# Attention by head pairs: block-diagonal keys and values, the bias factor in its band, and casts on GpSimd

## The chip, the cores and the metric

The kernel runs on one core of a Trainium2 chip. The metric is the device time of one execution in microseconds (us). The core has five engines that run side by side, each with an instruction queue of its own that is worked off in order: TensorE (PE in the profile, with its weight loads as PEld), VectorE (DVE), ScalarE (ACT), GpSimd (POOL) and SyncE (SP). SP, ACT and POOL can also start DMA transfers, which 16 DMA engines carry out.

## What is computed

Attention with a relative bias over 8 batches of 8 heads, 576 positions, head size 64, and behind it a mixture of experts in which a hash of the token's id picks one of 8 experts. Cut to what matters:

```python
scores = (1 / sqrt(D)) * q @ k.T + bias_table[bucket(|i - j|)]   # 8 x 8 heads, 576 x 576
attn = softmax(scores)                                           # over the keys j
x = (attn @ v), heads side by side                               # 4608 tokens x 512
e = token_ids * 2654435761 % 8                                   # one expert for each token
out[token] = relu(x[token] @ w1[e]) @ w2[e]                      # 512 -> 1024 -> 512
```

The bucket of a distance |i - j| grows up to 128, from there on it is the last one. Both kernels compute exp(score) times exp(bias), take the sum of a row from a column of ones beside the values, and divide at the end.

## The kernel before

**Setup** (lines 121 to 228). `tok`, `ident`, the one-hot table `ohsb` and the ids are loaded; a matmul makes the bias of every distance, ACT takes its exponential (`ebsb`), and it goes to DRAM (`t_ebp`). The token's rank within its expert is found by matmuls with a triangle and with ones; the result `ds2` is the row of `t_xperm` to which the token's `x` is to go. ACT's queue writes 5,140 KB of a fixed row over all expert slots of `t_xperm` (`zx`, line 301).

**Attention** (lines 232 to 430) runs over 8 batches `b` and in them over 4 head pairs `m`. SP loads `v` in float32 (`vb`), POOL loads `q` and `k` with a cast to float16 (`qb16`, `kb16`), 128 positions by 8 heads at a time. For each head a bias factor `ebias[h]` of 128 x 5 x 576 is read from DRAM, by way of a second DRAM array (`t_ebr`), in the first batch (`load_ebias`). For a pair PE transposes q and k (`psq`, `psk`), DVE copies them to `qT` and `kT` and casts v into `vaug` with its column of ones. The keys are cut into 5 tiles `t` of 128, 128, 128, 128 and 64. For each tile PE makes the scores of both heads (line 352: 64 rows of the array for a head, columns 512 and 64), ACT the exponential (line 360, 576 columns), DVE the product with `ebias` (line 368, 576 columns). Then for each head (line 393) 25 matmuls of 65 columns sum attn times v over the 5 key tiles for 5 chunks of queries; DVE takes reciprocals (line 406) and scales into `x_sb` (line 411). After a batch POOL sends 4 or 5 tiles of `x_sb` to their rows of `t_xperm` (line 420, "the dispatch").

**Experts** (lines 436 to 516): for each expert 640 rows are loaded from `t_xperm` (`xpn`, SP), transposed (`xps`), multiplied by `w1t` (`hps`, 512 matmuls of 320 columns in all) and `w2t` (`ops`, 320 of 512 columns), and POOL scatters the rows to the output. The change leaves these lines as they are. A branch behind them, for experts with over 640 tokens, is not entered.

What sets the order: the tile framework places the instructions of each engine in an order of its own and puts in the waits. Each DMA counts one of eight counters of its kind when it lands: `DMAHW0` to `DMAHW7` in turn for those from SP and ACT, `DMASW0` to `DMASW7` for those from POOL. The issue that comes to a counter again waits until the DMA before it on that counter has landed, and everything behind that issue in the same queue waits with it.

## Time and profile before

| | us |
|---|---|
| median of 3 runs | 644.87 (643.94 to 645.23) |
| the profiled execution | 647.33 |
| its span | 645.5 |
| PE busy | 526.1 |
| DVE busy | 315.6 |
| ACT busy | 245.3 |
| POOL busy | 159.3 |

The span is the stretch that the profile covers, and the sums below are made against it; the profiled execution took 1.8 us more than its span, the median 0.6 us less. A busy share is a mean over three stages with different limits: the setup up to about 96 us, the attention up to about 471 us, the experts behind it. So the profile is read stage by stage: what the chain of waits goes through there, and how long one instruction takes there.

### The profile page before, as it was taken

Reading aid. Unit: us, or ns where it says so; the run is one execution under the profiler, and the core shown is the slowest. Engines: PE = TensorE matmul, PEld = TensorE weight load, DVE = VectorE, ACT = ScalarE, POOL = GpSimd, SP = SyncE. Lnnn points to the kernel's source line nnn. Section 1 sums busy time; section 2 is a strip of 40 time slices with the busy share of each in tenths; the row PEclk is TensorE's granted clock in tenths of the full one; section 3 lists DMA queues with packets and bytes.
Section 4 is the critical chain, followed back from the end, with each engine's and each line's share of the span. In section 5 each row is a group of like instructions: output and inputs, shape, how many; then the busy total and the mean of one; then the engine's idle time right before and its main releaser. Section 6 shows DMA issues by size and latency. Waiting matters only on the chain.

```text
span 645.5 us, 9277 instructions
## 1 busy us (share of the span) xinstructions
PE 526.1 (82%) x3561; PEld 278.4 (43%) x3561; DVE 315.6 (49%) x1126; ACT 245.3 (38%) x386; POOL 159.3 (25%) x176
## 2 busy tenths in 40 slices
PE   2005149999999999999999999999919999999993
PEld 0002024454454454454454454454416655556661
DVE  0112036677676677676667666667612223322211
ACT  1004024445445445445545545545503322223330
POOL 5015310022232222232222330020020334423222
PEclk9999999999999999999999999999999999999997
DMA  9999999702912902911901910000032999999812
GB/s 149 184 152 164 235 269 246 167 35 18 130 43 13 134 34 14 135 42 11 136 34 11 137 43 1 1 34 1 1 95 79 196 218 212 218 187 205 183 73 82
DMA packets 147414, 69.74 MB, mean 108 GB/s; under 512 B 115155, under 2 KB 138743, under 8 KB 147360
## 3 DMA queue, kind: packets, MB, share of 16 engines
q0 software_dynamic: 92480, 40.40, 45.6%
q1 hardware_dynamic: 49744, 23.39, 16.2%
q10 hardware_dynamic: 5136, 5.26, 4.3%
q8 instruction: 30, 0.49, 0.3%
q14 instruction: 24, 0.20, 0.1%
HBM read 75.79 MB, written 22.99 MB: 153 GB/s over the span
## 4 chain that ended last, share of the span: by engine, by line
PE 63%; DMA 14%; issue 9%; ACT 8%; DVE 3%; POOL 1%; POOLq 0%; SPq 0%
PE px L393 21%; PE sc L352 14%; PE hps L478 11%; PE ops L496 11%; ACT attn L360 8%; DMA t_xperm<-zx 7%; PE psq L314 3%; DVE attn L368 2%; DMA ebias<-t_ebr 2%; PE psk L314 2%; DMA t_ebp<-ebsb 2%; PE xps L459 2%; DMA t_ebr<-t_ebp 1%; DMA vb<-in_v_dram 1%; POOL t_xperm L420 1%
## 5 line engine op out<-in xcount | busy, mean ns | idle before, releaser
L360 ACT ACTIVATE attn<-sc 128x576 f16<-128x576 f32 (+1 forms) x320 | 197.7, 648 | 257.0 <-PE sc L352 246.1
L393 PE MATMUL px<-vaug,attn 128*128 128x65 f16 (+3 forms) x1600 | 182.1, 243 | 24.7 <-DVE attn L368 22.0
L352 PE MATMUL sc<-qT,kT 64*128 64x512 f16 (+3 forms) x640 | 177.8, 428 | 22.9 <-ACT attn L360 22.6
L368 DVE TENSOR_TENSOR attn<-attn,ebias 128x576 f16<-128x576 f16 (+1 forms) x320 | 139.5, 452 | 93.4 <-ACT attn L360 56.0
L393 PEld LDWEIGHTS <-attn 128*128 128x128 f16 (+3 forms) x1600 | 117.4, 122 | 130.3 <-DVE attn L368 81.8
L484 ACT ACTIVATE h<-hps 128x640 f16<-128x640 f32 x64 | 45.1, 704 | 115.4 <-PE hps L478 115.0
L420 POOL DMA_INDIRECT t_xperm<-x_sb,ds x36 | 38.4, 1066 | 198.7 <-DVE x_sb L411 190.2
L352 PEld LDWEIGHTS <-kT 64*128 64x128 f16 (+1 forms) x640 | 46.6, 116 | 78.2 <-issue 68.0
L496 PE MATMUL ops<-w2t,h 128*128 128x512 f16 x320 | 72.7, 379 | 0.0
L478 PE MATMUL hps<-xpt,w1t 128*128 128x320 f16 x512 | 71.9, 301 | 0.0
L411 DVE TENSOR_SCALAR x_sb<-px,rcp 128x64 f16<-128x64 f32 (+1 forms) x320 | 70.0, 274 | 1.6
L274 POOL DMA_DIRECT2D qb<-in_q_dram x40 | 35.1, 878 | 131.1 <-PE psk L314 102.6
L478 PEld LDWEIGHTS <-w1t 128*128 128x128 f16 x512 | 50.4, 98 | 21.0 <-issue 0.2
L314 PE MATMUL psq<-ident,qb 128*128 128x128 f16 (+1 forms) x160 | 36.1, 292 | 21.9 <-DMA qb<-in_q_dram 15.2
L504 POOL DMA_INDIRECT out_dram<-ok,xpn x40 | 39.3, 981 | 56.5 <-DVE ok L503 54.4
L463 DVE COPY xpt<-xps 128x640 f16<-128x640 f16 x32 | 15.1, 489 | 73.6 <-PE xps L459 72.6
L503 DVE COPY ok<-ops 128x512 f32<-128x512 f32 x40 | 27.7, 692 | 47.0 <-PE ops L496 47.0
L314 PE MATMUL psk<-ident,kb 128*128 128x128 f16 (+1 forms) x160 | 36.5, 297 | 12.4 <-DMA kb<-in_k_dram 12.4
L496 PEld LDWEIGHTS <-h 128*128 128x128 f16 x320 | 30.7, 98 | 33.5
L406 DVE RECIPROCAL rcp<-px 64x1 f32<-64x1 f32 (+1 forms) x128 | 18.7, 166 | 50.6 <-PE px L393 47.8
L278 POOL DMA_DIRECT2D kb<-in_k_dram x40 | 35.2, 879 | 33.0 <-DMA kb<-in_k_dram 18.3
L314 PEld LDWEIGHTS <-qb 128*128 128x128 f16 (+1 forms) x160 | 19.8, 131 | 43.0 <-issue 26.1
(47 smaller groups left out, 138.6 us busy)
## 6 DMA issues: line engine op xcount, KB each, us to landing
vb<-in_v_dram SPq DMA_DIRECT2D x32, 256.0 KB, 5.1
w1t<-in_moe_w_dram POOLq DMA_DIRECT2D x8, 1024.0 KB
w2t<-in_moe_w_dram POOLq DMA_DIRECT2D x8, 1024.0 KB
ebias<-t_ebr SPq DMA_DIRECT2D x8, 720.0 KB, 7.5
t_xperm<-zx ACTq DMA_DIRECT2D x1, 5140.0 KB, 44.3
xpn<-t_xperm SPq DMA_DIRECT2D x8, 642.5 KB, 9.3
qb<-in_q_dram POOLq DMA_DIRECT2D x32, 128.0 KB
kb<-in_k_dram POOLq DMA_DIRECT2D x32, 128.0 KB
```

The costliest lines, as they stand in the source:

```text
L278: nc.gpsimd.dma_start(out=kb16[:nt, t, :, :], in_=k[b, :, P * t : P * t + nt, :].transpose([1, 0, 2]),)
L314: nc.tensor.transpose(out=pst[:, P * t : P * t + nt], in_=srct[:nt, t, 2 * m : 2 * m + 2, :], identity=ident[:nt, :nt],)
L352: nc.tensor.matmul(out=scps[hh][:nt, ns:ne], lhsT=kT[64 * hh : 64 * hh + 64, P * t : P * t + nt], rhs=qT[64 * hh : 64 * hh + 64, ns:ne], s ...
L360: nc.scalar.activation(out=attn[hh][:nt, t, :], in_=scps[hh][:nt, :], func=AF.Exp, bias=0.0, scale=scale,)
L368: nc.vector.tensor_tensor(out=attn[hh][:nt, t, :], in0=attn[hh][:nt, t, :], in1=ebias[2 * m + hh][:nt, NJT - 1 - t, :], op=ALU.mult,)
L393: nc.tensor.matmul(out=px[nbase : nbase + isz, c, :], lhsT=attn[hh][:nt, t, i0c : i0c + isz], rhs=vaug[hh][:nt, t, :], start=(imm == 0), s ...
L411: nc.vector.tensor_scalar(out=x_sb[nbase : nbase + isz, gt, h * D : (h + 1) * D], in0=px[nbase : nbase + isz, c, :D], scalar1=rcp[nbase : ...
L420: sc_in = nc.gpsimd.indirect_dma_start(out=xperm_d.ap()[:, :], out_offset=bass.IndirectOffsetOnAxis(ap=ds2[:, g : g + 1], axis=0), in_=x_s ...
L478: nc.tensor.matmul(out=hps[:, nr, :NR], lhsT=w1h[:, kt, ts(ft, P)], rhs=xt[e][:, kt, ts(nr, NR)], start=(kt == 0), stop=(kt == NPT - 1),)
L484: nc.scalar.activation(out=h1[:, ft, :].rearrange("p (r n) -> p r n", r=NRC), in_=hps[:, :, :NR], func=AF.Relu, bias=0.0, scale=1.0,)
L496: nc.tensor.matmul(out=ops[:, :], lhsT=h1[:, ft, ts(kc, P)], rhs=w2h[:, ft, :], start=(ft == 0), stop=(ft == NFT - 1),)
L504: so = nc.gpsimd.indirect_dma_start(out=out[:, :], out_offset=bass.IndirectOffsetOnAxis(ap=xn[e][:, kc, DM:XW].bitcast(I32), axis=0), in_= ...
```

## The change

Attention is written anew; the experts are not touched.

- **Pairs and block-diagonal keys.** `load(n)` loads q, k and v of one pair in float32 by eight DMAs of SP's queue; `cast_qk` and `cast_v` cast them to float16 on GpSimd. q and k are split into even and odd positions. `transposes(n)` makes 12 transposes of 96 x 128; DVE copies q to `qt`, and the keys of the two heads into the two diagonal blocks of `kz` (its other blocks are set to zero once). So one matmul with 128 rows gives the scores of 64 keys of either head: nine key tiles in all, eight of them taken in four groups `g` of 2 x 576 columns, and one of 576 (`scores`).
- **Values.** `va` holds the values of both heads in the same way, each head with its column of ones and zeros in the other's rows. Attn times v (`av_steps`) is 45 matmuls of 128 x 128 by 130 columns for a pair, in two PSUM tiles `px` of 27 and 18.
- **Bias in its band.** Distances of 128 and more have the last bucket; its factor cancels in the division. The table holds exp(bias - last bias), and DVE multiplies only the band around the diagonal: 7 operations with 512, 768, 512, 256, 256, 384 and 192 elements of a partition. Its table `ebd` is loaded by 16 DMAs, eight from SP and eight from ACT.
- **Order.** PE's order is written out: the scores of pair n between blocks of 12 matmuls of attn times v of pair n-1, and at the end the transposes of pair n+2. PSUM has two buffers `ps` of three banks, and two of one bank (`aux`) that `pq`, `pk` and `px` take in turn.
- **Dispatch.** 40 tiles go to `t_xperm`, five for each batch; routing (`route`) moves behind the second pair.

```diff
-                nc.gpsimd.dma_start(
-                    out=qb16[:nt, t, :, :],
-                    in_=q[b, :, P * t : P * t + nt, :].transpose([1, 0, 2]),
-                )
...
+        def aux(shape, dtype, name):
+            return atp.tile(shape, dtype, name=name, tag="aux", bufs=2,
+                            space=bass.MemoryType.PSUM)
...
+        kz = [at.tile([P, NCH, 2, D], F16, name=f"kz{i}") for i in range(3)]
+        va = [at.tile([P, NCH, VW], F16, name=f"va{i}") for i in range(4)]
+        ebd = at.tile([P, NPAIR, 2, 2, WB], F16, name="ebd")
...
+        def load(n):
+            b, m = pairs[n]
+            for dst, src, name in ((qf, q, "qf"), (kf, k, "kf")):
+                dst[n] = at.tile([PB, 2, NBLK, 2 * D], F32, name=name, bufs=4)
+                for hh in range(2):
+                    nc.sync.dma_start(
+                        out=dst[n][:, hh, :, :],
+                        in_=src[b, 2 * m + hh].rearrange(
+                            "(k p c) d -> p k (c d)", k=NBLK, c=2
+                        ),
+                    )
+            vf[n] = at.tile([P, NCH, D], F32, name="vf", bufs=4)
+            for hh in range(2):
+                for c in range(2):
+                    r0 = D * hh + HD * c
+                    nc.sync.dma_start(
+                        out=vf[n][r0 : r0 + HD, :, :],
+                        in_=v[b, 2 * m + hh].rearrange(
+                            "(x p c) d -> c p x d", c=2, p=HD
+                        )[c],
+                    )
+
+        def cast_qk(n):
+            for dst, src, name in ((qh, qf, "qh"), (kh, kf, "kh")):
+                dst[n] = at.tile([PB, 2 * NBLK, 2, D], F16, name=name, bufs=3)
+                nc.gpsimd.tensor_copy(
+                    out=dst[n][:, :, :, :].transpose([0, 2, 1, 3]),
+                    in_=src[n][:, :, :, :].rearrange(
+                        "p h k (c d) -> p h (k c) d", c=2
+                    ),
+                )
+
+        def cast_v(n):
+            for hh in range(2):
+                r0, r1 = D * hh, D * hh + D
+                nc.gpsimd.tensor_copy(
+                    out=va[n % 4][r0:r1, :, hh * (D + 1) : hh * (D + 1) + D],
+                    in_=vf[n][r0:r1, :, :],
+                )
+
+        for n in range(2):
+            load(n)
+
+        tbl = at.tile([NB, H], F32, name="tbl")
+        nc.sync.dma_start(out=tbl[:, :], in_=bias_table)
+        ohsb = at.tile([NB, FW], F32, name="ohsb")
+        nc.scalar.dma_start(out=ohsb[:, :], in_=OH_d.ap())
+        nc.sync.dma_start(out=ident[:, :], in_=I128_d.ap())
...
+        for i, x in enumerate(va):
+            for hh in range(2):
+                r0, r1 = D * hh, D * hh + D
+                o0, o1 = D - D * hh, P - D * hh
+                c0 = hh * (D + 1)
+                nc.gpsimd.memset(x[o0:o1, :, c0 : c0 + D + 1], 0.0)
+                nc.gpsimd.memset(x[r0:r1, :, c0 + D : c0 + D + 1], 1.0)
+            if i < 2:
+                cast_v(i)
...
+        nc.gpsimd.memset(zx[:, :DM], 0.0)
+        nc.gpsimd.memset(zx[:, DM:XW].bitcast(I32), BIG)
+
+        def fill_table():
+            nc.scalar.dma_start(
+                out=xperm_d.ap()[:NSLOT, :].rearrange("(p r) d -> p r d", p=P),
+                in_=zx[:, :].unsqueeze(1).to_broadcast([P, NSLOT // P, XW]),
+            )
+
...
+        def transposes(n):
+            b, m = pairs[n]
+            pq = aux([P, S], F16, "pq")
+            pk = aux([P, S], F16, "pk")
...
+            qt = at.tile([P, S], F16, name="qt", bufs=3)
+            nc.vector.tensor_copy(out=qt[:, :], in_=pq[:, :])
+            z = kz[n % 3]
+            for hh in range(2):
...
+        def scores(n, g):
+            b, m = pairs[n]
+            qt, z = qts[n], ktz[n]
+            ps = atp.tile([P, 3, 512], F32, name="ps", bufs=2,
+                          space=bass.MemoryType.PSUM)
+            if g == 0:
+                atts[n] = (
+                    at.tile([P, NDUO, 3, QW], F16, name="att", bufs=3),
+                    at.tile([P, S], F16, name="atts", bufs=3),
+                )
+            att, ats = atts[n]
+            if g < NDUO:
+                for c in range(2):
+                    kt = z[:, 2 * g + c, :, :].rearrange("p h u -> p (h u)")
+                    nc.tensor.matmul(
+                        out=ps[:, c, :QW], lhsT=kt, rhs=qt[:, :QW],
+                        start=True, stop=True,
+                    )
+                    nc.tensor.matmul(
+                        out=ps[:, 2, RW * c : RW * c + RW], lhsT=kt,
+                        rhs=qt[:, QW:], start=True, stop=True,
+                    )
+                nc.scalar.activation(
+                    out=att[:, g, :, :], in_=ps[:, :, :QW],
+                    func=AF.Exp, bias=0.0, scale=scale,
+                )
...
+                    nc.vector.tensor_tensor(
+                        out=a, in0=a,
+                        in1=ebd[:, m, :, :, a0 + w0 : a1 + w0], op=ALU.mult,
+                    )
...
+        def av_steps(n):
+            b, m = pairs[n]
+            att, ats = atts[n]
+            vb = va[n % 4]
+            for its in ((0, 1, 2), (3, 4)):
+                px = aux([P, len(its), 2, D + 1], F32, "px")
+                todo = [(ii, it, t) for ii, it in enumerate(its)
+                        for t in range(2 * NDUO + 1)]
+                for x, (ii, it, t) in enumerate(todo):
...
+                    nc.tensor.matmul(
+                        out=px[:, ii, :, :].rearrange("p h d -> p (h d)"),
+                        lhsT=lhsT, rhs=vb[:, t, :],
+                        start=(x == 0), stop=(x == len(todo) - 1),
+                        skip_group_check=True,
+                    )
+                    if x < len(todo) - 1:
+                        yield
+                ni = len(its)
+                rcp = at.tile([P, 3, 2], F32, name="rcp", bufs=4)
+                nc.vector.reciprocal(out=rcp[:, :ni, :], in_=px[:, :, :, D])
+                nc.vector.tensor_tensor(
+                    out=x_all[:, b, its[0] : its[0] + ni,
+                              P * m : P * m + P].rearrange(
+                        "p t (h d) -> p t h d", h=2
+                    ),
+                    in0=px[:, :, :, :D],
+                    in1=rcp[:, :ni, :].unsqueeze(3).to_broadcast(
+                        [P, ni, 2, D]
+                    ),
+                    op=ALU.mult,
+                )
+                yield
...
+        def dispatch(b):
+            for t in range(NIT):
                 sc_in = nc.gpsimd.indirect_dma_start(
                     out=xperm_d.ap()[:, :],
                     out_offset=bass.IndirectOffsetOnAxis(
+                        ap=ds2[:, B * t + b : B * t + b + 1], axis=0
                     ),
+                    in_=x_all[:, b, t, :],
                     in_offset=None,
+                    bounds_check=NROW - 1,
+                    oob_is_err=False,
                 )
                 disjoint(sc_in, "xrows")
+
+        def advance(it, count):
+            for _ in range(count):
+                if next(it, "end") == "end":
+                    return
+
+        NP = len(pairs)
+        with tc.manual_schedule(engines={mybir.EngineType.PE}):
+            transposes(0)
+            transposes(1)
+            for n in range(NP + 1):
+                av = av_steps(n - 1) if n > 0 else iter(())
+                if n < NP:
+                    if n + 2 < NP:
+                        load(n + 2)
+                        cast_qk(n + 2)
+                        cast_v(n + 2)
+                    for g in range(NIT):
+                        scores(n, g)
+                        if g < NDUO:
+                            advance(av, 12)
+                    advance(av, 99)
+                    if n + 2 < NP:
+                        transposes(n + 2)
+                    if n == 1:
+                        fill_table()
+                        route()
+                    if n == 4 * 5:
+                        load_w1(0)
+                        load_w2(0)
+                else:
+                    advance(av, 99)
+                if n > 0 and pairs[n - 1][1] == NPAIR - 1:
+                    dispatch(pairs[n - 1][0])
+            load_w1(1)
+            load_w2(1)
```

How the framework places this shows at three places. The first is SP's queue at the start; names in square brackets are the counters waited for. Before:

```order
L142 DMA sltsb<-t_slt 128x128
L148 DMA er<-in_moe_token_ids_dram 36x256
L268 DMA vb<-in_v_dram 128x8x64
L268 DMA vb<-in_v_dram 128x8x64 [waits DMAHW0_49]
L268 DMA vb<-in_v_dram 128x8x64 [waits DMAHW1_49]
```

and in the changed kernel, from the last loads of pair 1 on:

```order
L180 DMA vf<-in_v_dram 32x9x64 [waits DMAHW6_49]
L180 DMA vf<-in_v_dram 32x9x64 [waits DMAHW7_49]
L180 DMA vf<-in_v_dram 32x9x64 [waits DMAHW0_49]
L180 DMA vf<-in_v_dram 32x9x64 [waits DMAHW1_49]
L209 DMA tbl<-in_bias_table_dram 32x8 [waits DMAHW2_49]
L212 DMA ident<-t_ident 128x128 [waits DMAHW3_49]
L264 DMA tok<-t_tok 128x40 [waits DMAHW4_49]
```

The DMA that counts `DMAHW7` for the first time is the fill of `t_xperm`, which the framework has put second on ACT's queue, behind the memset of `zx`; `tbl` and `ident`, which went first, now stand behind the issue that waits for it. The four loads of weights that `load_w1` and `load_w2` issue in the attention stand early on POOL's queue, among the casts of pairs 0 and 1.

The second place is POOL's queue around a dispatch. Before, the loads of q and k of a batch to come stand on either side of it:

```order
L278 DMA kb_1369<-in_k_dram 64x8x64 [waits DMASW1_49]
L420 DMA t_xperm<-x_sb,ds_60 9728x514 [waits DMAHW3_49,DMASW2_49,DVE_49]
L420 DMA t_xperm<-x_sb,ds_60 9728x514 [waits DMASW3_49,DVE_49]
L420 DMA t_xperm<-x_sb,ds_60 9728x514 [waits DMASW4_49,DVE_49]
L420 DMA t_xperm<-x_sb,ds_60 9728x514 [waits DMASW5_49,DVE_49]
L274 DMA qb_1966<-in_q_dram 128x8x64 [waits DMASW6_49,PE_49]
```

In the changed kernel, at the dispatch of batch 0 (`va_79` here is that of pair 5, the `qh` and `kh` behind are those of pair 6, and the other six dispatches that have pairs behind them stand in the same way):

```order
L200 CAST va_79<-vf 64x9x64 [waits DMAHW6_49,DMAHW5_49,PE_49]
L517 DMA t_xperm<-x_all,ds_59 9728x514 [waits DVE_49]
L517 DMA t_xperm<-x_all,ds_59 9728x514 x2
L517 DMA t_xperm<-x_all,ds_59 9728x514 [waits DVE_49]
L200 CAST va_79<-vf 64x9x64 [waits DMASW7_49,DMASW6_49,DMAHW0_49,DMASW5_49,DMAHW7_49,DMASW4_49,Pool_49]
L517 DMA t_xperm<-x_all,ds_59 9728x514 [waits DMASW0_49,Pool_49]
L190 CAST qh<-qf 96x2x6x64 [waits DMAHW2_49,DMAHW1_49]
L190 CAST kh<-kf 96x2x6x64 [waits DMAHW4_49,DMAHW3_49]
```

The casts of pair 6 have moved behind the dispatch of batch 0, and between its fourth and fifth transfer stands a cast that waits until the first four have landed (`DMASW4` to `DMASW7`).

The third place is DVE's queue in one pair. Before:

```order
L368 TENSOR_TENSOR attn<-attn,ebias_143 64x576
L368 TENSOR_TENSOR attn<-attn,ebias_144 64x576
L321 COPY qT<-psq 128x576
L322 COPY kT<-psk 128x576
L406 RECIPROCAL rcp<-px 64x1
L406 RECIPROCAL rcp<-px 128x4
L411 TENSOR_SCALAR x_sb<-px,rcp 64x64
L411 TENSOR_SCALAR x_sb<-px,rcp 128x64 x4
```

and in the changed kernel, from the product of group 1 of a pair n on:

```order
L452 TENSOR_TENSOR att<-att,ebd 128x768
L501 RECIPROCAL rcp<-px 128x6
L502 TENSOR_TENSOR x_all<-px,rcp 128x3x128
L452 TENSOR_TENSOR att<-att,ebd 128x4x128
L452 TENSOR_TENSOR att<-att,ebd 128x4x64
L501 RECIPROCAL rcp<-px 128x4
L502 TENSOR_TENSOR x_all<-px,rcp 128x2x128
L452 TENSOR_TENSOR att<-att,ebd 128x4x64
L452 TENSOR_TENSOR att<-att,ebd 128x384
L469 TENSOR_TENSOR atts<-atts,ebd 128x192
L401 COPY qt<-pq 128x576
L404 COPY kz_76<-pk 64x9x64 x2
```

Ten products of 576 elements have become seven smaller ones, the two drains of `px` (pair n-1) have moved in between them, and the copies of the transposes (pair n+2) stand behind the last product.

## Rows read from the trace of the kernel before

**Rows 1.** Page, the span in 40 slices; a digit is a busy share in tenths.

```profile
PE   2005149999999999999999999999919999999993
PEclk9999999999999999999999999999999999999997
```

**Rows 2.** Chain of waits up to the first attn times v: start, us, what.

```profile
1.64 44.27 DMA t_xperm<-zx
45.92 7.11 DMA vb<-in_v_dram
...
78.07 14.78 DMA ebias<-t_ebr
95.76 2.10 PE px L393 x21
```

**Rows 3.** Chain of waits, attn times v of two pairs that follow each other.

```profile
296.58 4.39 PE px L393 x42
...
308.68 4.39 PE px L393 x42
```

**Rows 4.** Line L478 in two windows: ns min/median/max, first and last start.

```profile
L478 PE MATMUL hps<-xpt,w1t x5: 458/471/471, 486.9 to 488.5; 128*128 128x320 f16 x5
L478 PE MATMUL hps<-xpt,w1t x59: 296/299/327, 488.7 to 496.8; 128*128 128x320 f16 x59
```

**Rows 5.** Timeline of PE in narrow windows: start, us from first start to last end.

```profile
308.18 0.40 PE L393 MATMUL px<-vaug,attn 128*128 128x65 f16 x4
308.68 0.78 PE L393 MATMUL px<-vaug,attn 64*128 64x65 f16 x6
485.10 1.01 PE L459 MATMUL xps<-ident,xpn 128*128 128x128 f16 x8 [14.23 <-DMA xpn<-t_xperm]
515.43 0.72 PE L459 MATMUL xps<-ident,xpn 128*128 128x128 f16 x10
```

**Rows 6.** Groups by form: busy us, mean ns of one, idle before.

```profile
L360 ACT ACTIVATE attn<-sc 128x576 f16<-128x576 f32 x256 | 156.6, 649 | 243.9 <-PE sc L352 235.9 <-PE px L393 2.9 <-issue 1.5
L484 ACT ACTIVATE h<-hps 128x640 f16<-128x640 f32 x64 | 45.1, 704 | 115.4 <-PE hps L478 115.0 <-issue 0.3
L368 DVE TENSOR_TENSOR attn<-attn,ebias 128x576 f16<-128x576 f16 x256 | 111.2, 453 | 72.4 <-ACT attn L360 36.0 <-DMA ebias<-t_ebr 30.8 <-issue 1.3
L321 DVE COPY qT<-psq 128x576 f16<-128x576 f16 x32 | 14.2, 442 | 7.1 <-PE sc L352 5.5 <-PE psq L314 1.6
L406 DVE RECIPROCAL rcp<-px 128x4 f32<-128x4 f32 x64 | 11.7, 183 | 27.2 <-PE px L393 24.4 <-PE sc L352 1.8
L203 DVE TENSOR_REDUCE rank<-inc 128x36 f32<-128x288 f32 x1 | 0.6, 631 | 0.0
L198 DVE TENSOR_TENSOR inc<-inc,rps 128x288 f32<-128x288 f32 x1 | 0.5, 454 | 0.0
L224 DVE TENSOR_TENSOR dlt<-dlt,ovf 128x36 f32<-128x36 f32 x1 | 0.2, 194 | 0.0
L327 DVE CAST vaug<-vb 128x256 f16<-128x256 f32 x64 | 18.4, 288 | 26.8 <-DMA vb<-in_v_dram 26.8
```

**Rows 7.** SP's waits: us in total, times, longest.

```profile
SPq L268 <- DMA t_xperm<-zx: 22.1, 1, 22.1
```

**Rows 8.** Two stretches: us, busy us of PE, PEld, DVE, ACT, POOL, granted clock, DMA share, GB/s.

```profile
12.00:56.00 44.00, 4.67 (x21) 1.90 (x21) 7.18 (x36) 0.00 (x0) 10.31 (x13) 1.00 1.56 166
60.00:98.00 38.00, 14.67 (x86) 6.35 (x85) 6.07 (x22) 7.95 (x13) 7.88 (x9) 1.00 1.26 242
```

**Rows 9.** Timeline at the end of the attention.

```profile
465.95 4.92 PE L393 MATMUL px<-vaug,attn 128*64 128x65 f16 x46
475.69 0.96 POOL L420 DMA_INDIRECT t_xperm<-x_sb,ds  x1 [0.30 <-issue]
476.95 0.96 POOL L420 DMA_INDIRECT t_xperm<-x_sb,ds  x1 [0.30 <-issue]
480.01 1.51 SPq L445 DMA_DIRECT2D xpn<-t_xperm  x3
```

545 lines of the change are left out of this document (249 added, 296 removed).

## The prediction

> **What bounds it now.** I read the page's slices first, for the stages. PE is busy to nine tenths in nearly every slice from about 100 us on, apart from a dip where the attention ends and the first slices of the setup [rows 1]. So I took the chain of waits in each stage.
>
> In the setup it runs through a transfer, not an engine: the fill of `t_xperm` is issued at 1.6 us and lands at 45.9; the loads of `vb` stand behind it on SP, by a counter that they share with it, for 22.1 us [rows 7]; then come `vb` and the bias factors, and the first attn times v starts at 95.76 [rows 2]. In the attention the chain is PE's own: attn times v of one pair starts at 296.58, of the next at 308.68, so 12.1 us for a pair [rows 3], 32 times over.
>
> PE is slower there than its busy digits tell. The clock row says 9 throughout, but the first five matmuls of line 478 take 471 ns and the 59 behind them 299, the change falling at 488.7 [rows 4]; eight transposes take 1.01 us at 485.1, ten take 0.72 at 515.4 [rows 5]. Four attn times v of 65 columns take 0.40 us [rows 5], against 0.11 for 260 columns at 2.4 GHz. So I take it that the attention runs at the lower level (1.2 GHz), and that only the row of matmuls without a gap from 485.1 on, 3.6 us long, ended at the upper. The matmul of 64 rows also starts 0.50 us after the first of the four before it [rows 5], 0.1 us after their end: a change of tile shape costs PE about that, and the changed kernel has far fewer.
>
> At the end the last attn times v ends at 470.87; the dispatch starts a transfer every 1.27 us (0.96 and 0.30 of pause), and SP loads the first `xpn` 3.06 us after the last one's start, at 480.01 [rows 9]. From there to the end of the span, 165.5 us, nothing is changed.
>
> **PE's pair after.** Scores: 4 x 1152 + 576 = 5184 columns, 2.2 us at 2.4 GHz. Attn times v: 45 x 130 = 5850 columns, 2.5 us. Twelve transposes: 1.0, by the ten in 0.72 [rows 5] with some room. Sum 5.7 us at the upper level, about 10.3 at the lower. I take the upper: the blocks of 12 matmuls fill PE's waits for ACT, all attn times v tiles are of one shape, and 488.7 shows that PE gets there when nothing interrupts it.
>
> **ACT.** 576 elements take 649 ns and 640 take 704 [rows 6]: 0.86 ns an element and 154 fixed. Four of 1152 at 1.15 and one of 576 make 5.2 us (before 6.5).
>
> **DVE.** 36 float32 elements take 194 ns, 288 take 454: 1.03 ns an element, 157 fixed; 576 float16 products take 453, so 0.51 an element [rows 6]. Seven products with 2880 elements: 1.1 + 1.5 = 2.6. Three copies out of PSUM at 0.44: 1.3. Two reciprocals at 0.18, and two products with `px` of 384 and 256 elements, 0.55 and 0.42: 1.3. Sum 5.2 us.
>
> **The pair's loop.** These sums lie side by side, but PSUM ties them: `px` takes the bank that the copy of q left, and that copy stands behind all products of the pair on DVE. From it: 27 matmuls of attn times v with two groups of scores between, 1.5 + 1.0 on PE; then DVE in order the drain of `px` (0.73), products of group 2 (0.71), second drain (0.60), groups 3 and 4 (0.90), the copy of q (0.44): 3.4. Together 5.9 us for a pair, without handing over. I put 0.65 us for the handovers and as much for DVE operations that GpSimd holds up; neither has a row, and both are my choice between 5.9 (neither) and 9.3 (DVE waits for all casts, below). **Taken: 7.2 us.**
>
> **GpSimd's casts.** No row of before shows a GpSimd cast. A pair casts 2 x 768 + 2 x 576 = 2688 elements of a partition in four operations. The nearest rows are DVE's: the cast at 288 ns for 256 elements (0.51 an element) gives 2.0 us; the float32 product (1.03) 3.4; the reduction with its stride, 631 ns for 288 (1.65), 5.1 [rows 6]. I take 3.4, since the operands are float32 and strided. A dispatch adds 5 x 1.27 in four pairs, 1.6 for each; 5.0 is under 7.2. The Trainium skill ("GPSIMD Engine Reference", § 3.1 on elementwise operations) gives some 1.8 cycles an element at best; an estimate from that at 1.2 GHz is 4.0 us a pair, which no trace so far shows and which would leave the sum as it is.
>
> **Loads.** Eight DMAs a pair on SP, 0.9 MB, in place of the loads that cast on POOL's queue: over 7.2 us that is 123 GB/s, below the 166 and 242 that the two stretches of setup moved [rows 8]; two pairs ahead, so I cost it at nothing. If it were not hidden it would be 0.9 MB at 166 GB/s, 5.3 us a pair, still under the period.
>
> **The start.** The fill now waits on POOL for casts and memsets, so it is issued at about 10 us instead of 1.6. Beside it run 4.2 MB of weights. 9.4 MB take 39 us at 242 GB/s and 57 at 166 [rows 8], so the landing lies between 44 (the fill ahead of the weights) and 67; I take 51. `tbl` and `ident` stand behind the issue that waits for it, as `vb` did [rows 7]. Then 4.5 us for `ident` and `tbl` (between the 3.06 of a dispatch row and the 7.11 of `vb` [rows 2, 9]), 4.5 for `t_f`, and 15 for the 16 loads of `ebd`, by the 14.78 of `ebias` [rows 2]: first attn times v at 75, against 95.76. The first pair at the lower level and the routing, whose operations stand on DVE between two pairs, take 14: **the second at 89.**
>
> **Dispatch.** The casts of pair 4b+6 stand on POOL behind the dispatch of batch b. From the first drain of `px`: four transfers, 4 x 1.27 less the last pause of 0.30, are 4.8; the cast of v in front of the fifth waits for the landing of the fourth, 2.1 more (3.06 less 0.96 [rows 9]), so 6.9; that cast takes 0.75, the fifth transfer 1.27, two casts of q and k 0.95 each: 10.8. PE comes to the transposes of that pair some 1.5 us after the drain, so it waits 9.3 us, and DVE and ACT with it, since PE's order is fixed. Then PE starts at the lower level, as after the 14.23 us of waiting at 485.1 [rows 5]; 3.6 us at half speed lose 1.8, a whole pair 4.6; I take 2.5. **11.8 a batch, 7 batches: 82.6.** This is the term that I am least sure of in size. Before, casts in the DMA did not stand in that way.
>
> **Sum.** 89 + 30 x 7.2 (216) + 82.6 + last attn times v 2.6 + last dispatch and landing 8.1 (4 x 1.27 + 3.06) + 165.5 = 563.8, as a span beside 645.5. The profiled execution took 1.8 more than its span, the median 0.6 less; against the median **563 us**.
>
> **Rivals.** *PE stays at the lower level.* For it: it did through the whole attention before, though busy to nine tenths; against: the shapes no longer change, and PE has more to do in place of its gaps. A pair is then 10.5, the stop 7.6 (the casts have more lead and no clock is lost): 89 + 315 + 53 + 5 + 8 + 165.5 = 635.
>
> *GpSimd and DVE shut each other out.* If every cast holds up DVE for its full length, the loop is 5.9 + 3.4 = 9.3: 89 + 279 + 82.6 + 2.6 + 8.1 + 165.5 = 627. Against: no row of before has both engines on computing work, so there is nothing for it either. The Trainium skill ("SBUF — State Buffer", § on the two separate sides) states such a lock: a DVE operation with two SBUF inputs and a GpSimd operation that reads SBUF can't run together, the loser waits for the whole instruction. No trace so far shows it; it speaks against this change.
>
> *Slower than before: the casts bound.* POOL's pair is C + 2.2, its casts and a quarter of the 8.9 us up to the end of the fifth transfer. 265.2 + 30 x (C + 2.2) reaches 645 at C = 10.5 us, 3.9 ns an element all in. That is over twice the dearest row (1.65), which is DVE's; GpSimd's own elementwise rate has no row. At C = 12 the time is 690.
>
> *The stops don't bite.* The fill lands at 44, and the stop is 5 us with no loss of clock, because `qh` and `kh` come earlier than I count or PE has work to spare: 82 + 216 + 35 + 2.6 + 8.1 + 165.5 = 509.
>
> **How the numbers follow.** My forecast has 0.55, with 525 to 600 as its own range (a pair at 6.3 to 8.0 us, a batch's stop at 8 to 14); the lower clock 0.14, the lock 0.14, the casts 0.05, no stops 0.12. The range from 505 to 636 takes in the forecast, the lock, the 509, and half of the lower clock; outside are the other half (0.07), the casts (0.05) and tails (0.06). About 0.2% is what a measurement of this kernel can tell from no change. Slower has the casts' 0.04 above that bound, same 0.01, faster 0.95.
>
> **What would show it.** In the profile after: line 491 starting every 57 ns (upper level) or 108 (lower); the fill landing near 51 and SP waiting on it ahead of `tbl`; the first line 491 near 75; PE idle some 9 us seven times, its chain going through POOL's line 517 to the casts of line 190; a GpSimd cast of 768 elements at 0.95 us, of 576 at 0.75; products of line 452 at 0.55 for 768 elements, and longer where a cast runs beside. It would be wrong if the casts take over 2 us each, if PE's pitch within a batch is over 9 us, or if the waits at the dispatch belong to something else than POOL's queue.

## The result and the profile after

The changed kernel takes 544.39 us (median of 4 runs, 543.42 to 545.91) against 644.98 before: a ratio of 0.8445 with a 95% interval of 0.8423 to 0.8467. The profiled execution took 544.60, its span is 542.7. The prediction was 563 with a range from 505 to 636.

PE's digits and the granted clock of the page (PEclk, in tenths of 2.4 GHz), which answer to [rows 1]:

```profile
PE   0000736928938658469389387492799999999992
PEclk9999957968959959879879689697799999999997
```

PE starts after a tenth of the span and then stops every 37.6 us: the dips to 2, 3 and 4. Here the clock's row follows them; before it said 9 throughout.

The chain of waits in the setup (start, us, what), for [rows 2]:

```profile
8.53 42.79 DMA t_xperm<-zx
...
59.42 10.26 DMA t_f<-ebsb
69.70 2.22 DMA ebd<-t_f
71.94 1.79 DMA ebd<-t_f
```

The fill lands at 51.3. Behind it SP issues `tbl`, PE and ACT make `ebsb`, and its copy to `t_f`, issued at 59.4, takes 10.3 us.

The timeline of PE, for [rows 3] and [rows 5]: start, us from first start to last end, and in brackets the idle time before with what ended it:

```profile
76.35 0.87 PE L491 MATMUL px<-va,att 128*128 128x130 f16 x4 [7.68 <-DVE att L452]
...
109.64 0.63 PE L491 MATMUL px<-va,att 128*128 128x130 f16 x8
110.11 0.22 PE L491 MATMUL px<-va,atts 128*128 128x130 f16 x1
110.16 0.41 PE L459 MATMUL ps<-qt,kz 128*128 128x288 f16 x2
120.11 0.66 PE L386 MATMUL pq<-ident,qh 96*128 96x96 f16 x6 [9.54 <-POOL qh L190]
...
122.30 1.07 PE L491 MATMUL px<-va,att 128*128 128x130 f16 x8
```

The first attn times v starts at 76.35. At 110 the eight matmuls run at the upper level: 0.63 us with 0.22 for one by itself, so 59 ns from start to start. Then PE stands for 9.54 us, until a cast of q ends; after that eight such matmuls take 1.07, the lower level.

The timeline of GpSimd at that stop, for [rows 9]:

```profile
110.29 1.20 POOL L517 DMA_INDIRECT t_xperm<-x_all,ds  x1 [11.52 <-DVE x_all L502]
111.79 1.02 POOL L517 DMA_INDIRECT t_xperm<-x_all,ds  x1 [0.31 <-issue]
113.11 0.97 POOL L517 DMA_INDIRECT t_xperm<-x_all,ds  x1 [0.30 <-issue]
114.39 0.97 POOL L517 DMA_INDIRECT t_xperm<-x_all,ds  x1 [0.30 <-issue]
117.26 0.68 POOL L200 CAST va<-vf 64x576 f16<-64x576 f32 x1 [1.90 <-DMA t_xperm<-x_all,ds]
118.22 0.98 POOL L517 DMA_INDIRECT t_xperm<-x_all,ds  x1 [0.28 <-POOL va L200]
119.24 0.82 POOL L190 CAST qh<-qf 96x768 f16<-96x768 f32 x1
120.00 0.82 POOL L190 CAST kh<-kf 96x768 f16<-96x768 f32 x1
```

It is the chain of the prediction, link by link. Over the attention it comes back as the main wait of PE (engine, line, what it waited for, us in total, times, longest); seven of the eight are the stops, of 9.0 to 9.5 us, 9.2 in the mean:

```profile
PE pq L386 <- POOL qh L190: 65.5, 8, 9.5
```

The groups by form (busy us, mean ns of one, idle before), for [rows 6]:

```profile
L436 ACT ACTIVATE att<-ps 128x1152 f16<-128x1152 f32 x128 | 144.3, 1130 | 147.0 <-issue 80.8 <-PE ps L432 41.0 <-ACT atts L464 12.5
L200 POOL CAST va<-vf 64x576 f16<-64x576 f32 x64 | 45.8, 716 | 103.2 <-DMA vf<-in_v_dram 56.8 <-PE px L491 32.3 <-DMA t_xperm<-x_all,ds 12.7
L190 POOL CAST qh<-qf 96x768 f16<-96x768 f32 x32 | 28.1, 879 | 12.7 <-DMA qf<-in_q_dram 11.1
L452 DVE TENSOR_TENSOR att<-att,ebd 128x768 f16<-128x768 f16 x32 | 18.5, 579 | 40.0 <-ACT att L436 40.0
L502 DVE TENSOR_TENSOR x_all<-px,rcp 128x384 f16<-128x384 f32 x32 | 17.9, 558 | 1.1
L401 DVE COPY qt<-pq 128x576 f16<-128x576 f16 x32 | 14.4, 451 | 67.3 <-PE pq L386 67.3
```

ACT's 1152 elements (1.13 us, put at 1.15), the products (0.58 for 768; put at 0.55), the drain (0.56; 0.55) and the copy (0.45; 0.44) came out as worked out from [rows 6]; the casts are a little cheaper than put: 0.88 and 0.72 in the mean, 0.82 and 0.66 to 0.68 where nothing disturbs them, so 3.0 us a pair in place of 3.4.

### The profile page after: what moved, and what is told of

It reads as the page before. It is cut to its first block, busy times and chain, and to the rows that moved or that the text cites. A ratio compares the mean times of both kernels' runs of the same rounds, so it can differ in the third digit from the quotient of the medians.

```text
span 542.7 us, 8776 instructions
## 1 busy us (share of the span) xinstructions
PE 364.1 (67%) x3403; PEld 267.1 (49%) x3403; DVE 216.0 (40%) x553; ACT 208.8 (38%) x226; POOL 197.5 (36%) x248
## 4 chain that ended last, share of the span: by engine, by line
PE 31%; issue 28%; DMA 20%; POOL 13%; SPq 4%; DVE 1%; ACT 1%; POOLq 1%; ACTq 0%
PE hps L607 13%; PE ops L625 13%; DMA t_xperm<-zx 8%; DMA t_xperm<-x_all,ds 6%; POOL va L200 5%; POOL kh L190 4%; POOL t_xperm L517 3%; PE px L491 2%; DMA t_f<-ebsb 2%; PE xps L588 2%; SPq L180 2%; SPq L170 1%; DMA vf<-in_v_dram 1%; DMA kf<-in_k_dram 1%; PE ps L428 1%
## 5 line engine op out<-in xcount | busy, mean ns | idle before, releaser
L436 ACT ACTIVATE att<-ps 128x1152 f16<-128x1152 f32 x128 | 144.3, 1130 | 147.0 <-issue 80.8
L491 PE MATMUL px<-va,att 128*128 128x130 f16 x1280 | 114.2, 237 | 16.1 <-DVE att L452 8.1
L491 PEld LDWEIGHTS <-att 128*128 128x128 f16 x1280 | 98.1, 107 | 31.1 <-issue 14.6
L452 DVE TENSOR_TENSOR att<-att,ebd 128x512 f16<-128x512 f16 (+1 forms) x192 | 76.9, 430 | 58.2 <-ACT att L436 56.7
L428 PE MATMUL ps<-qt,kz 128*128 128x384 f16 x256 | 83.8, 365 | 1.1 <-ACT att L436 1.1
L200 POOL CAST va<-vf 64x576 f16<-64x576 f32 x64 | 45.8, 716 | 103.2 <-DMA vf<-in_v_dram 56.8
L517 POOL DMA_INDIRECT t_xperm<-x_all,ds x40 | 39.3, 982 | 109.0 <-DVE x_all L502 80.6
L432 PE MATMUL ps<-qt,kz 128*128 128x192 f16 x256 | 68.6, 268 | 0.0
L633 POOL DMA_INDIRECT out_dram<-ok,xpn x40 | 39.2, 979 | 57.4 <-DVE ok L632 51.3
L491 PE MATMUL px<-va,atts 128*128 128x130 f16 x160 | 37.1, 232 | 0.3 <-ACT atts L464 0.3
L428 PEld LDWEIGHTS <-kz 128*128 128x128 f16 x256 | 27.6, 108 | 11.6 <-issue 4.7
```

What stands on the lines that cost most here:

```text
L200: nc.gpsimd.tensor_copy(out=va[n % 4][r0:r1, :, hh * (D + 1) : hh * (D + 1) + D], in_=vf[n][r0:r1, :, :],)
L428: nc.tensor.matmul(out=ps[:, c, :QW], lhsT=kt, rhs=qt[:, :QW], start=True, stop=True,)
L432: nc.tensor.matmul(out=ps[:, 2, RW * c : RW * c + RW], lhsT=kt, rhs=qt[:, QW:], start=True, stop=True,)
L436: nc.scalar.activation(out=att[:, g, :, :], in_=ps[:, :, :QW], func=AF.Exp, bias=0.0, scale=scale,)
L452: nc.vector.tensor_tensor(out=a, in0=a, in1=ebd[:, m, :, :, a0 + w0 : a1 + w0], op=ALU.mult,)
L491: nc.tensor.matmul(out=px[:, ii, :, :].rearrange("p h d -> p (h d)"), lhsT=lhsT, rhs=vb[:, t, :], start=(x == 0), stop=(x == len(todo) - 1 ...
```

## The experiments

Beside the experiments the kernel before ran at 648.2 to 648.5 us, so times are compared by ratio to it where a few us matter. "A pair" is the distance from one start of the transposes of q to the next. In the changed kernel a batch is four of them: 15.5 us with the stop in it, then 7.1 and 9.2 or 8.5 and 7.2, then 6.14, the undisturbed pair.

**e1: GpSimd's order.**

```diff
-        with tc.manual_schedule(engines={mybir.EngineType.PE}):
+        with tc.manual_schedule(
+            engines={mybir.EngineType.PE, mybir.EngineType.Pool}
+        ):
```

> The changed kernel with GpSimd's instructions kept in the order in which the code is written, so that the casts of pair 4b+6 stand ahead of the dispatch of batch b and no cast stands between its transfers; the weights are issued early as in the changed kernel. Theory (GpSimd's order makes the stop): behind the dispatch now stand the casts of pair 4b+7, which PE wants one pair later; five transfers 6.4 us and two casts 1.7 are 8.1 us from the first drain of px, PE comes to them about 1.5 + 6.15 = 7.7 us after it, so a stop of 9.5 us shrinks to under 1.5; no clock is lost behind it; a batch takes 26 to 29 us in place of 37.9, and the time is 465 to 490. Rival (the transfers themselves, or DVE, hold PE whatever the order): the stops stay at about 9 us, 540 to 548.

The same edit issues the four loads of weights ahead of the loop over the pairs. Measured: 512.25 us, ratio 0.789 (0.786 to 0.792). The stop of over 9 us is gone; what is left of it is a wait of up to 1.7 us for a cast of k. So the order makes the stop. But a batch takes 32 to 33 us (9.1, 9.0 to 10.4, 7.2, 6.55), not 26 to 29: the pair with the dispatch and the one behind it stay long. Half of the gain went somewhere that neither theory named.

**e2: the fill from another queue.**

```diff
-            nc.scalar.dma_start(
+            nc.gpsimd.dma_start(
                 out=xperm_d.ap()[:NSLOT, :].rearrange("(p r) d -> p r d", p=P),
```

> The changed kernel with the fill of t_xperm issued from GpSimd's queue, at the same place among memsets and casts, so that no counter of SP's and ACT's transfers is held by it. Theory (SP waits for the fill's landing by the counter, not for bandwidth): SP issues tbl and ident at about 10 us, the first attn times v starts at 35 to 45 in place of 76.4, and the time falls by 30 to 42, to 502 to 515; the first dispatch must not come before the fill lands. Rival (the fill and the weights take the DMA engines, and every small load is late with them): the first attn times v stays above 65, 533 to 546.

Measured: 542.53 us, ratio 0.837 (0.835 to 0.839): next to nothing. SP's timeline:

```profile
18.49 0.82 SPq L243 DMA_DIRECT2D t_f<-ebsb  x1
21.79 18.12 SPq L180 DMA_DIRECT2D vf<-in_v_dram  x1
55.08 11.86 SPq L254 DMA_DIRECT2D ebd<-t_f  x8
```

`tbl` is issued at 8.8 us and `t_f` at 18.5, as expected, but the loads that wait for `t_f` come at 55.1, and SP stands 18 us at a load of v for a counter. The fill is under way until 47.1 here, and `t_f` (384 KB) is late by the traffic beside it. The rival holds: the counter was one of two covers of the same 40 us.

**e3: no casts.**

```diff
-                        cast_qk(n + 2)
-                        cast_v(n + 2)
+                        qh[n + 2], kh[n + 2] = qh[n % 2], kh[n % 2]
...
-            vb = va[n % 4]
+            vb = va[n % 2]
```

> The changed kernel without the casts of pairs 2 to 31: PE reads the float16 q, k and v of pairs 0 and 1 again and again (the loads stay). Theory (GpSimd's casts make both the stop and the long pairs behind it, by standing behind the dispatch and by holding up DVE): a batch is four pairs of 6.15 us, 24.6 to 26, and the time 445 to 460; no product of line 452 with 512 elements lasts over 0.5 us. Rival A (the stop is the casts' but the long pairs behind it come from PE's lower clock alone): the same time, since without a stop the clock isn't lost, but the long products of 1.0 us stay. Rival B (the dispatch itself holds PE): over 520.

Measured: 486.71 us, ratio 0.751 (0.749 to 0.753). No product of 512 elements lasts over 427 ns, and two pairs of a batch take 6.14. But the pair at the dispatch takes 9.2 to 10.7 and the one behind it 5.9 to 7.4, with no cast anywhere near. The timeline of PE and ACT there (the dispatch's five transfers start at 284.41 to 289.51):

```profile
287.50 0.25 PE L432 MATMUL ps<-qt,kz 128*128 128x192 f16 x1
...
292.81 0.32 PE L428 MATMUL ps<-qt,kz 128*128 128x384 f16 x1 [2.37 <-ACT att L436]
...
286.58 1.13 ACT L436 ACTIVATE att<-ps 128x1152 f16<-128x1152 f32 x1 [0.95 <-ACT atts L464]
291.63 3.17 ACT L436 ACTIVATE att<-ps 128x1152 f16<-128x1152 f32 x3 [3.92 <-remote]
```

PE has the scores of group 1 done at 287.75, ACT is free at 287.71, and its exponential starts at 291.63. The trace's record of semaphore updates tells why: PE's semaphore, on which ACT waits, is raised as follows (us; ends of the matmuls that raise it, then the updates on record):

```
matmul ends   286.26   287.74   288.93   289.10
updates       286.51   291.61   291.77   291.82
```

PE's updates come up to 3.9 us late, all at once, when the fifth transfer begins to land. It is so at each of the seven dispatches within the attention.

**e4: mixed tile shapes.**

```diff
+                    rhs = vb[:, t, :]
+                    if t == 2 * NDUO:
+                        lhsT, rhs = lhsT[:D], rhs[:D]
                     nc.tensor.matmul(
                         out=px[:, ii, :, :].rearrange("p h d -> p (h d)"),
-                        lhsT=lhsT, rhs=vb[:, t, :],
+                        lhsT=lhsT, rhs=rhs,
```

> The changed kernel with the ninth key tile of attn times v cut to its first 64 rows of the array (the last 64 keys of the second head are left out): five of a pair's 45 matmuls have another shape, as five in 25 of the kernel before. It asks why PE ran at 1.2 GHz through the attention before. Theory 1 (changing shapes costs pauses that keep PE at the lower level): line 491 starts every 108 ns through whole batches, a pair takes over 9 us, and the time is over 600. Theory 2 (a change of shape costs some 0.1 us and no more, the level is the gaps' doing): line 491 stays at 57 ns away from the stops, ten changes make a pair 6.5 to 7.2 us, and the time 555 to 580.

Measured: 560.96 us in one run. The undisturbed pair takes 6.98, so ten changes of shape cost 0.84 us, 84 ns each (95 by PE's starts, 154 ns apart at a change in place of 59), and PE stays at the upper level there (eight matmuls in 0.63 us). Theory 2.

**e5: the dispatch without GpSimd** (from e3).

```diff
-                sc_in = nc.gpsimd.indirect_dma_start(
-                    out=xperm_d.ap()[:, :],
...
+                r0, p0 = S * b + P * t, 0 if t < NDUO else NB4 + P - S
+                sc_in = nc.sync.dma_start(
+                    out=xperm_d.ap()[r0 : r0 + P - p0, :],
+                    in_=x_all[p0:, b, t, :],
+                )
```

> The kernel of e3 (no casts of pairs 2 to 31) with its dispatch sent by SP's queue as plain transfers to fixed rows, 576 rows a batch, so that tokens go to the wrong experts; the same bytes leave x_all. In e3 each dispatch still cost about 4.4 us: one pair of 10.6 us among pairs of 6.14, in which PE's updates of its semaphore come up to 3.9 us late. Theory (GpSimd's indirect transfers hold those updates back): every pair takes 6.1 to 6.5 us, no update is over 0.5 us late, and the time falls by some 30 us to 452 to 462. Rival (the traffic out of x_all, or the writes, are what disturbs, whoever sends them): pairs of 9 to 10 us stay, 480 to 490.

Measured: 451.18 us in one run. Every pair from the fourth on takes 6.14 or 6.15, and no update is late. So in e3 it went with GpSimd's indirect transfers, not with the bytes; the two ran on different chips, which e9 comes back to.

**e6: PE kept busy at the stop.**

```diff
+                    if n >= 4 and n % 4 == 0:
+                        dps = atp.tile([P, 3, 512], F32, name="ps", bufs=2,
+                                       space=bass.MemoryType.PSUM)
+                        for _ in range(58):
+                            nc.tensor.matmul(
+                                out=dps[:, 0, :QW],
...
                     if n + 2 < NP:
                         transposes(n + 2)
```

> The changed kernel with 58 more matmuls of 384 columns on PE at the place of each of the seven stops (their result is read by nobody), 9.3 us at the upper level, so that PE runs while it waits for the casts. Theory (PE's lower clock behind the stop is a cost of its own, 2.5 us by the prediction): the stops stay, the two long pairs behind them fall from 16.2 us together to some 13.5 to 14, and the time by 14 to 20, to 524 to 531. Rival (the pairs behind the stop are long because the casts that run in a burst there hold up DVE): under 6 us, 538 to 546.

Measured: 545.70 us, ratio 0.842 (0.839 to 0.845), the same as without. The timeline of PE:

```profile
112.28 9.59 PE L554 MATMUL ps<-qt,kz 128*128 128x384 f16 x58 [0.45 <-ACT att L436]
121.70 0.42 PE L386 MATMUL pq<-ident,qh 96*128 96x96 f16 x6
...
129.63 0.41 PE L395 MATMUL pk<-ident,kh 96*128 96x96 f16 x6 [1.85 <-DVE x_all L502]
131.65 1.02 PE L491 MATMUL px<-va,att 128*128 128x130 f16 x8 [1.11 <-DVE qt L401]
```

The pair behind the stop runs at the upper level and takes 5.3 to 5.9 us in place of 7.0 to 8.6, but then PE waits for DVE, falls back to the lower level (the last line), and the next pair takes 8.4 to 11.2 in place of 7.2 to 9.2. Together the two take 15.4 us in the mean, against 16.0, and the pair with the stop 16.2, against 15.5. So holding the clock up alone gains nothing. That doesn't clear the clock. Three stretches of the changed kernel (us, busy us of PE, PEld, DVE, ACT, POOL, granted clock, DMA share, GB/s), the two pairs behind a stop and an undisturbed one:

```profile
158.17:166.68 8.51, 8.37 (x75) 7.03 (x76) 3.89 (x10) 3.94 (x4) 7.10 (x9) 0.62 0.84 216
166.70:173.87 7.17, 5.65 (x77) 4.81 (x75) 5.71 (x15) 5.06 (x6) 3.00 (x5) 1.00 0.78 197
136.47:142.61 6.14, 5.65 (x77) 4.81 (x75) 4.68 (x15) 5.06 (x6) 0.65 (x1) 1.00 0.18 53
```

The first pair is PE's, for the most part at its lower clock: it is busy all but 0.14 us. The second has the full clock and four casts beside it; DVE is busy 1.03 us longer than in the undisturbed pair, and the pair is as much longer. In e6, where the clock is held up, the casts of the burst hold DVE instead: each of the two covers part of the other.

**e7: full rows in the kernel before.**

```diff
-                                lhsT=kT[64 * hh : 64 * hh + 64,
-                                        P * t : P * t + nt],
-                                rhs=qT[64 * hh : 64 * hh + 64, ns:ne],
+                                lhsT=kT[hh][:, P * t : P * t + nt],
+                                rhs=qT[:, ns:ne],
```

> One part of the change alone, in the kernel before: the keys of the two heads of a pair stand in two tiles with zeros in the other head's rows, so that the matmuls of line 352 use all 128 rows of the array; columns, casts, bias and order stay. It asks why PE ran at 1.2 GHz through the attention of the kernel before. Theory (half-filled arrays kept it there): line 393 starts every 28 ns or so, a pair takes 8 to 9.5 us (DVE's and ACT's sums) in place of 12.1, and the time is 530 to 570. Rival (it is PE's waits for ACT, whatever the rows): 12 us a pair, 640 to 655.

Measured: 664.35 us in one run, slower than before (648.4 beside it) and above both ranges. The clock's row of its page:

```profile
PEclk9999555766556575556855555675557999999998
```

The attention stays mostly at the lower level (0.58 granted from 100 to 470 us), and here the record shows it. Half-filled arrays alone were not the reason.

**e8: put together.** e1 with loads and casts three pairs ahead, `tbl` and `ident` first, routing ahead of the scores, and the fill in larger pieces, issued behind the casts of the first pairs:

```diff
-        zx = at.tile([P, XW], F16, name="zx")
+        ZR = 8
+        zx = at.tile([P, ZR, XW], F16, name="zx")
...
-            nc.scalar.dma_start(
-                out=xperm_d.ap()[:NSLOT, :].rearrange("(p r) d -> p r d", p=P),
+            nc.gpsimd.dma_start(
+                out=xperm_d.ap()[:NSLOT, :].rearrange(
+                    "(p k r) d -> p k (r d)", p=P, r=ZR),
```

> GpSimd's order as written, loads and casts three pairs ahead, table and identity loaded first, the fill in rows of 8 KB from GpSimd's queue behind the casts of the first pairs, routing ahead of the first scores, weights late. Theory (start bound by the traffic of the fill ahead of t_f and ebd, stops by GpSimd's order): the first attn times v at 30 to 40, no pair waits for a cast, a batch 28 to 31 us with 4 us of it at the dispatch, the time 445 to 470. Rival (the loads of the pairs fall behind when fill and weights run beside them): the first batches take over 35 us, and the time stays above 485.

Measured: 441.37 us, ratio 0.680 (0.675 to 0.684). The first attn times v starts at 33.9; the fill is issued behind it, at 40.7, and the first weights at 175.8. A batch takes 28 to 30 us, but not as expected: the pair with the dispatch takes 6.14 but for the first (7.7), with no update late; the two behind it, beside which the casts run that stood behind the dispatch, take 6.7 to 10.

**e9: other counter numbers** (from e3).

```diff
+        tbl = at.tile([NB, H], F32, name="tbl")
+        nc.sync.dma_start(out=tbl[:, :], in_=bias_table)
+        ohsb = at.tile([NB, FW], F32, name="ohsb")
+        nc.scalar.dma_start(out=ohsb[:, :], in_=OH_d.ap())
+        nc.sync.dma_start(out=ident[:, :], in_=I128_d.ap())
         for n in range(2):
             load(n)
```

> The kernel of e3 (no casts of pairs 2 to 31, dispatch by GpSimd) with table and identity loaded first on SP. By that the framework numbers its counters in another order: PE's and ACT's semaphores come ahead of those of GpSimd's transfers (108 and 110, with 111 to 118 for the transfers), not behind them (117 and 118, with 109 to 116). In e8, which has the same numbers, no update of PE's came late at a dispatch and the pairs there took 6.14 us. Theory (the late updates hang on these numbers): all pairs from the third on take 6.1 to 6.6 us, and the time falls by 30 besides what the start gives (0 to 45), to 410 to 457. Rival (e8 was spared by something else, its order or its loads): one pair of 9 to 10.7 us at every dispatch, the attention after the start as long as in e3.

Measured: 452.50 us, ratio 0.698 (0.695 to 0.701). Of the 34 us less than in e3, 4.4 are the start (first attn times v at 75.4, against 79.8). The pair at the dispatch takes 6.14 to 6.20. ACT's timeline there, with the transfers from 254.07 to 260.15:

```profile
256.00 1.13 ACT L435 ACTIVATE att<-ps 128x1152 f16<-128x1152 f32 x1 [0.71 <-ACT atts L463]
257.44 3.50 ACT L435 ACTIVATE att<-ps 128x1152 f16<-128x1152 f32 x3 [0.31 <-PE ps L431]
```

The instructions and transfers at this place are those of e3; only the order of the first loads of the setup differs, and the 4.4 us a batch are gone. What differs at that place is the numbers of the counters, and the chip: e1 and e3 ran on one chip, e5 and e8 on a second, e9 and e12 on a third, and no version with late updates was run on two. So it isn't shown that the numbers are the cause. The kernel before speaks against them as the whole of it: there PE's and ACT's semaphores (116 and 117) stand behind those of GpSimd's transfers (99 to 106) too, and at its dispatches every update on record follows its matmul within 0.1 us.

**e10 and e11: DVE's share.** e10 leaves the products out. e11 takes all columns:

```diff
-                    a0, a1 = max(u0, lo), min(u1, hi)
-                    if a0 >= a1:
-                        continue
+                    a0, a1 = lo, hi
```

> The changed kernel without the products with the bias table (lines 452 and 469 left out), so 2.6 us less on DVE for a pair. Theory (the undisturbed pair is bound by the loop through PSUM, in which DVE has 1.6 us of them): the undisturbed pair falls from 6.14 to PE's own 5.5 to 5.7, the stops stay at 9.5 us, the time is 515 to 532. Rival (PE alone bounds the pair): 6.1 us stays, 536 to 545.

> The changed kernel with the products over all columns, nine of them with 5184 elements in place of seven with 2880 (the table's entries don't belong there, so scores are weighted wrongly): the part of the change that cuts the bias to its band is undone. 2 x 0.157 + 2304 x 0.51 are 1.5 us more on DVE for a pair. Theory (DVE's products stand in the loop): an undisturbed pair takes 7.2 to 7.8 us, the time is 570 to 595, so that the band is worth 30 to 50 us. Rival (DVE has that much to spare): under 6.5 us a pair, 541 to 555.

Measured, one run each: 525.32 us with an undisturbed pair of 5.82, a little over the 5.5 to 5.7 worked out, and 580.57 with one of 6.6 to 7.0. In e10 the pairs behind the stop fall to 7.6 and 5.82; the first is PE's lower clock again (granted 0.71, PE busy for 7.5 us of it). The band is worth some 36 us. Less than worked out comes in the undisturbed pair (0.5 in place of 1.5): of the 2304 elements more, only 1280 stand in groups 2 to 4, the part of DVE's order that the loop runs through, 0.65 us at 0.51 ns. The rest comes at the stop (16.3 to 16.8) and in the pairs beside casts, which rise to 8.6 and 9.2 to 11.0.

**e12: e8 with earlier weights.**

```diff
+                    if n == 4 * 6:
+                        load_w1(1)
+                        load_w2(1)
...
-            load_w1(1)
-            load_w2(1)
```

> The kernel of e8 with the second expert's weights issued at pair 24 in place of behind the last dispatch, where in e8 they ran beside the first xpn, which took 12.8 us to land and kept PE waiting 20.8 us, against 13.6 in the changed kernel. Theory: the wait falls to 12 to 14 us and the time by 6 to 8, to 432 to 437. Rival (loads of pairs 26 on fall behind the weights): no gain, 440 to 446.

Measured: 432.38 us, ratio 0.667 (0.665 to 0.670). PE's wait at the end of the attention, in e8 and then in e12:

```profile
281.25 2.02 PE L597 MATMUL xps<-ident,xpn 128*128 128x128 f16 x15 [20.75 <-DMA xpn<-t_xperm]
```

```profile
268.63 2.02 PE L598 MATMUL xps<-ident,xpn 128*128 128x128 f16 x15 [13.18 <-DMA xpn<-t_xperm]
```

It is the fastest version of this study, a fifth below the changed kernel by the ratios (0.667 to 0.8445).

## Why the prediction was right, and where its steps were off

The prediction held in direction, range and mechanism; the time lies 19 us under the forecast, by terms of the pair that were mis-sized. By its steps:

| | predicted | measured |
|---|---|---|
| fill lands | 51 | 51.3 |
| first attn times v | 75 | 76.4 |
| the same of the second pair | 89 | 91.6 |
| undisturbed pair | 7.2 | 6.14 |
| PE's stop at a dispatch | 9.3 | 9.2 (9.0 to 9.5) |
| lost behind a stop | 2.5 | 3.8 |
| a batch | 40.6 | 37.6 |
| last attn times v to the end | 173.6 | 173.3 |

**The start** is right to 3 us, with luck: 51 for the fill was a choice between 44 and 67, and behind it errors stand against each other. `t_f` was issued 8.1 us after the fill had landed, not 4.5, and took 10.3, not 4.5 (9.8 in e8, with neither fill nor weights beside it); from there to the first attn times v were 6.7 us, not the 15 of the far larger `ebias`. The step that SP's counter makes the wait was half of the truth: e2 takes the counter away and gains nothing, since the traffic holds the same transfers. e8, which moves fill and weights behind the start, gains 42 us there; that its fill goes in larger pieces has no part in this.

**The dispatch** is the term that I called least sure in size, and it was the best: 9.0 to 9.5 us in each of seven batches, with the landing wait in the middle (1.90 measured, put at 2.1). e1 shows that the order on GpSimd is its cause.

**The pair's loop** failed in size. Its sum from PE and DVE was 5.9; I added 0.65 for handovers and 0.65 for casts that hold DVE, and charged both to every pair. The undisturbed pair is 6.14: the handovers are 0.24. The casts don't stand beside every pair; the stop drives them into bursts. So the 0.65 was wrong in place, and over four pairs the two terms were 4.2 us too much. The loss behind the stop, which I put down to PE's clock alone (2.5), is 3.8, so 1.3 too little. Where the pairs are of 8.5 and 7.2 us, 2.4 of it stand in the pair in which PE is busy throughout at the lower clock, near what I put, and 1.0 are casts beside a pair at the full clock, which I had spread over all pairs (the rows under e6). But e6 holds the clock up and gains nothing, since the casts then hold DVE; e3 removes casts and stops together, so it can't part the two. All this makes the 3 us a batch, 21 in all, by which the forecast was too high. e10 and e11 bear the loop out: less DVE work shortens the undisturbed pair, more lengthens it.

**The lock** of the rival is there, at part of its price. DVE's timeline in the changed kernel, products of 512 and 256 elements without a cast beside them and with one, and GpSimd's:

```profile
103.78 0.62 DVE L452 TENSOR_TENSOR att<-att,ebd 128x512 f16<-128x512 f16 x2
...
126.76 1.67 DVE L452 TENSOR_TENSOR att<-att,ebd 128x512 f16<-128x512 f16 x2
```

```profile
126.66 0.82 POOL L190 CAST kh<-kf 96x768 f16<-96x768 f32 x1
127.43 1.59 POOL L200 CAST va<-vf 64x576 f16<-64x576 f32 x2
```

Of the 64 products of 512 elements, 51 have no cast beside them and take 427 ns at most; of the other 13, seven take no longer and six 895 to 1,049, at most about one cast of 0.66 us more. That agrees with the lock that the Trainium skill states ("SBUF — State Buffer", § on the two separate sides) for a product with two SBUF inputs beside a GpSimd operation that reads SBUF. The rival's price, the whole 3.4 us on every pair, did not come: four casts of 3.0 us in all made the pair of 7.17 us 1.03 longer, so most of their time fell where DVE was not held.

**The clock.** That PE ran at the lower level before and reaches the upper one now holds: 59 ns between matmuls of 130 columns, and 108 behind a stop. (The 0.40 us of [rows 5], which the prediction set against 0.11, holds the length of the last matmul, 0.24; from start to start the four are 52 ns apart, so the reading stands.) Two of my reasons for the lower level fell: neither tile shapes that change (e4) nor half-filled arrays (e7) bring it about alone. What remains is the many short waits of PE for ACT in the kernel before; no run changed those alone, so it stays open.

**The rivals.** PE at the lower level: no. The casts as the bound: no, 3.0 us a pair. The stops that don't bite: no, they bit; e1, in which GpSimd's order is mended, took 512 us, near that rival's 509, but it has late updates where the rival counted 5 us of stop, so the nearness is luck.

## What to carry to other kernels

Where work moves onto an engine's queue, read the order that results around the rare, slow instructions there: casts that stood behind five transfers and a landing stopped PE for 9.2 us at each dispatch (65 in all), while four casts beside a pair's products cost it 1.0. An engine's stop can hide a second cost that comes out when the stop is mended, as the late updates did in e1, so judge such a repair by the pitch of the loop and not by the vanished wait. And before a slow clock behind a stop is counted as a gain to be had, keep the engine busy through it, as e6 did: a second cost lay under it, and nothing was gained.

## What was not expected of the hardware

- At each dispatch within the attention PE's semaphore updates came up to 3.9 us late in e3 and up to 3.3 in e1, and not at all in e8, e9 and e12. In the first two PE's semaphore has number 117 and ACT's 118, behind those of GpSimd's transfers; in the others 108 and 110, ahead of them. In the kernel before they stand behind as well (116 and 117), with no update on record late, and the first two ran on another chip than the others. So the cause stays open. In the changed kernel, with 117 and 118, PE stands still during the transfers, so that nothing shows.
- While a fill of 5,140 KB was under way, `t_f`, 384 KB and 0.8 us of issue, was followed by its readers only 36.6 us later in e2; in e8, with no fill beside it, by 9.8.
- A change of tile shape on PE costs 84 ns (e4), near the 0.1 us that [rows 5] gave.
- A GpSimd cast from float32 takes 0.82 us for 768 elements and 0.66 for 576. That is 0.83 ns for one more element, below the 1.8 cycles (1.5 ns at 1.2 GHz) of the estimate from the Trainium skill ("GPSIMD Engine Reference", § 3.1 on elementwise operations). The same section of the Trainium skill also gives 1.03 cycles, 0.86 ns, for its shortest loop bodies; the measurement lies near that.
